# Eight left-over final products of a fused top-k attention and SMeLU kernel: three, three and two behind the next chunk's first pairs, instead of two behind each of four

## The chip, the cores and the metric

The kernel runs on one core of a Trainium2 chip. The metric is the device time of one execution in microseconds (us); lower is better. A profiled execution gives, beside its time, the span from its first to its last instruction and a trace of the engines: PE (TensorE, matmuls) with PEld (its weight loads), DVE (VectorE), ACT (ScalarE), POOL (GpSimd) and SP (SyncE, which issues the DMAs).

## What is computed

Eight batches of eight heads, 576 tokens, head size 64, all in fp32. First an attention that keeps, for each query, the 32 largest scores; then, on its 4608 rows of 512, a two-layer network with a smooth rectifier between the layers:

```python
scores = np.matmul(q, k.transpose(0, 1, 3, 2)) / np.sqrt(D)
kth = np.partition(scores, -32, axis=-1)[..., -32:-31]
scores = np.where(scores >= kth, scores, -1e9)
attn = softmax(scores)
x = np.matmul(attn, v)                    # brought to (4608, 512)
h = x @ w_in                              # w_in: 512 x 2048
g = np.where(h >= 1, h, np.where(h <= -1, 0, (h + 1) ** 2 / 4))
out = g @ w_out                           # w_out: 2048 x 512
```

## The kernel before

**Steps and chunks.** The attention goes in 144 steps; a step is one pair of heads of one tile of 128 queries (the 64 left-over queries of two batches share a tile). Four steps make a chunk of 128 rows of `x`, kept transposed in `xT`. There are 36 chunks, numbered here from 0 to 35; each then goes through the network.

**A step.** PE makes the scores (L327, tile `sp`), ACT scales and copies them to `s` (L329). DVE finds the 32nd largest score of each row with MAX8 and MATCH_REPLACE8 (L342 to L421), ACT makes the exponentials `e` in two halves (L363 `nmax`, L365), and DVE masks and sums them (L428). POOL divides by the sum (L381). ACT splits the weights into 16-bit halves (L458), a DMA writes them out as `rows` (L460), a transposing DMA brings them back as `wT` (L461), and PE multiplies them with the values (L475, L483, tile `po`), two steps after the step's own DVE work. ACT copies the result to `xT` (L488, L490). In the first dozen steps, while the network's weights are still being converted on ACT, DVE and POOL, and in the last two, PE transposes instead (L443, L449).

**A chunk in the network** (`mlp`, L499). Sixteen blocks f of 128 hidden units go in eight pairs x = 0 to 7 (`GROUP = 2`; the last chunk takes them singly). `hidden(x)` makes the **first products** of a pair, eight matmuls into the PSUM tile `ph` (three buffers, shared with `po`), which the trace shows as 16 records. ACT makes `r` (L512) and `g` (L519) of it, POOL finishes `g` (L524, L525, L526); `g` has eight buffers. `final(f)` makes one **final product** (L531): it adds block f of `g` times `w_out` into the PSUM tile `py`, and the trace shows two records. `py` has one buffer (`bufs=1`, L530). After final product 15, ACT copies `py` to `y` (L534) and SP sends it to `out` (L536).

**The order.** It is written by a planner when the program is built, and each engine goes through its own instructions in that order (`manual_schedule`). `mlp` is called when the values of a chunk's last step are issued and appends the chunk's work to the list `pending`: pairs x = 0 to 7, and the final products of pair x behind pair x + 4 (`LAG = 4`). So eight final products, 8 to 15, stand behind the last pair; they carry a mark (the fourth entry). When the next chunk comes, the marked ones that are still at the end of the list are taken off it into `behind` (L540 to L542) and mixed in between its first pairs. `advance` (L604) takes work from the head of the list, in seven slots a step: a pair costs 8 units, a final product 4, and a slot hands out a share that the step sets from the work that is left. In slot 2 come the values of two steps ago and the scores of two steps ahead; ACT's exponentials stand in slots 3 and 4, `halves` in slot 3, the `parts` copies for turned queries and keys in slot 1. ACT's copy to `y` and SP's DMA are issued with final product 15, wherever that falls.

Of the kernel before, what the change touches and what calls it, by code (L numbers as in the profile page):

```python
# [24 lines left out]
def kernel(  # L25
# [28 lines left out]
    GROUP = 2  # L54
# [59 lines left out]
    def needed(f, second):  # L114

        return (f // n_in) * (NK + n_in * n_out) + NK + (n_out * (f % n_in + 1) if second else 0)
# [54 lines left out]
    def run(ctx, paired):  # L171
# [327 lines left out]
        def mlp(xT, rows, pool, last):  # L499
            gs, group = {}, 1 if last else GROUP  # L500
            py = []

            def hidden(x):
                ph = ps.tile([P, group, P], F32, name="ph", tag="ph", bufs=3)
                for i in range(group):
                    f = x * group + i
                    for kk in range(NK):
                        nc.tensor.matmul(ph[:, i], w_in[:, kk, f * P:(f + 1) * P], xT[:, kk],  # L508
                                         start=(kk == 0), stop=(kk == NK - 1))

                r = pool.tile([P, GROUP, P], F32, name="r", bufs=2)[:, 0:group]
                nc.scalar.activation(r, ph, AF.Relu, bias=half, scale=0.5)  # L512
                gs[x] = g = pool.tile([P, GROUP, P], F32, name="g", bufs=2 * LAG)[:, 0:group]
                if last:
                    nc.vector.tensor_scalar(g, ph, -1.0, 0.0, ALU.add, ALU.max)
                    nc.scalar.activation(r, r, AF.Square)
                    nc.vector.scalar_tensor_tensor(out=g, in0=r, scalar=1.0, in1=g, op0=ALU.min, op1=ALU.add)
                    return
                nc.scalar.activation(g, ph, AF.Relu, bias=minus, scale=1.0)  # L519
                if converted < n_pieces and x % 2:  # L520
                    nc.scalar.activation(r, r, AF.Square)
                    nc.gpsimd.tensor_scalar(r, r, 1.0, 0.0, ALU.min, ALU.max)
                else:
                    nc.gpsimd.tensor_scalar(r, r, 1.0, 0.0, ALU.min, ALU.max)  # L524
                    nc.gpsimd.tensor_tensor(out=r, in0=r, in1=r, op=ALU.mult)  # L525
                nc.gpsimd.tensor_tensor(out=g, in0=r, in1=g, op=ALU.add)  # L526

            def final(f):
                if f == 0:
                    py.append(ps.tile([P, DM], F32, name="py", tag="py", bufs=1))  # L530
                nc.tensor.matmul(py[0], gs[f // group][:, f % group], w_out[:, f, :], start=(f == 0), stop=(f == NF - 1))  # L531
                if f == NF - 1:
                    y = (late or words).tile([P, DM], F32, name="y", bufs=1)
                    nc.scalar.copy(y, py[0])  # L534
                    for p0, p1, dst in rows:
                        nc.sync.dma_start(out=dst, in_=y[p0:p1])  # L536

            behind = []  # L540
            while pending and pending[-1][3]:
                behind.insert(0, pending.pop())  # L542
            for x in range(NF // group + LAG):
                if x < NF // group:
                    pending.append((NK * group, needed(x * group + group - 1, False), partial(hidden, x), False))
                if x < LAG:
                    for _ in range(min(GROUP, len(behind))):
                        pending.append(behind.pop(0)[0:3] + (False,))
                else:
                    for f in range((x - LAG) * group, (x - LAG + 1) * group):  # L550
                        pending.append((DM // P, needed(f, True), partial(final, f), x >= NF // group))
# [142 lines left out]
        def values_until(m):  # L694
            nonlocal valued, pe_time
            while valued < min(m, n):
                pe_time = max(pe_time, ready_at[valued]) + 1.25
                values(state[valued])
                state[valued] = None
                if valued in ready:  # L700
                    ch = ready[valued]
                    mlp(xTs[ch], rows_of(*chunks[ch]), mlp_pool, ch == len(chunks) - 1)
                valued += 1
# [117 lines left out]
```

## Time and profile before

| | us |
|---|---|
| median of 3 runs | 1583.9 (1581.3 to 1587.99) |
| profiled execution, its own time | 1578.63 |
| span of the profiled execution | 1576.8 |
| ACT busy in the span | 1162.1 |
| POOL busy in the span | 939.0 |
| first products on PE (L508), busy | 571.7 |
| final products on PE (L531), busy | 556.2 |
| scores on PE (L327, main form), busy | 163.0 |
| copies to `y` (L534), 36 of them, busy | 20.9 |

Busy time is time in which an engine executes an instruction; a matmul's end is modelled, so the start of the next one tells more than its end. A line of the timeline gives the start in us from the span's start, the length, the engine, the line of the kernel, the operation, the tiles written and read, the shapes and how many were merged; in brackets, if the engine was idle before it, for how long and what ended that. A line of the waits reads: who <- for what: us in all, how many times, the longest.

### The profile page before, as it was taken

To read this page: it belongs to the slowest core of one execution; us is meant where nothing else is said; L and a number is where in the kernel's file an instruction comes from. 1 tells how busy PE (TensorE), PEld (TensorE's weight loads), DVE (VectorE), ACT (ScalarE), POOL (GpSimd) and SP (SyncE) were. 2 spreads that over 40 slices of the span, in tenths; PEclk is the share of its full clock that TensorE was granted. 3 is DMA by queue.
4 is the path that set the end of the run, shared out by engine and by line. 5 is a ranking of instruction groups with operands and counts; after the bars stand their busy time and mean duration, and the time that the engine had idled before them with its cause. 6 is when DMAs were issued, how large, how long until landed. Compare 5 with 4: busy or idle time off the path is not lost.

```text
span 1576.8 us, 32399 instructions
## 1 busy us (share of the span) xinstructions
PE 1481.3 (94%) x10685; PEld 1056.7 (67%) x10685; DVE 1432.2 (91%) x4443; ACT 1162.1 (74%) x2278; POOL 939.0 (60%) x1376
## 2 busy tenths in 40 slices
PE   5587899999999999999999999999999999999998
PEld 4465667677777676666666766666777666777775
DVE  6999989999999999989998999989999999999912
ACT  5677667787778877777777877777778777777732
POOL 4766466566666556655666655566666665666630
PEclk6799999999999999999999999999999999999999
DMA  9433245866577767885576776676566866655610
GB/s 253 131 97 99 61 125 149 219 188 154 161 192 199 199 158 169 217 202 146 161 184 181 198 177 166 190 206 180 161 172 190 201 177 156 169 158 154 138 43 16
DMA packets 504626, 256.25 MB, mean 163 GB/s; under 512 B 451712, under 2 KB 459904, under 8 KB 504448
## 3 DMA queue, kind: packets, MB, share of 16 engines
q1 hardware_dynamic: 504448, 254.08, 61.0%
q8 instruction: 87, 1.43, 0.4%
q14 instruction: 91, 0.75, 0.2%
HBM read 62.91 MB, written 100.27 MB: 103 GB/s over the span
## 4 chain that ended last, share of the span: by engine, by line
PE 79%; ACT 8%; DMA 5%; DVE 4%; issue 2%; POOL 1%; ACTq 0%; DVEq 0%; POOLq 0%; SPq 0%
PE ph L508 29%; PE py L531 28%; PE sp L327 10%; PE po L475 9%; ACT halves L458 2%; DMA rows<-halves 2%; DMA wT<-rows 2%; PE pw L443 1%; PE po L483 1%; ACT e L365 1%; DVE bits L147 1%; DMA lines<-parts 1%; DVE more L349 1%; ACT s L329 1%; ACT r L512 1%
## 5 line engine op out<-in xcount | busy, mean ns | idle before, releaser
L508 PEld LDWEIGHTS ph<-xT,w_in 128*128 128x128 f32 x4608 | 555.8, 192 | 133.7 <-issue 100.4
L531 PE MATMUL py<-w_out,g 128*128 128x512 f32 x1152 | 556.2, 601 | 19.6 <-ACT y L534 19.6
L508 PE MATMUL ph<-xT,w_in 128*128 128x128 f32 x4608 | 571.7, 278 | 2.6 <-ACT xT L488 2.6
L524 POOL TENSOR_SCALAR r<-r 128x256 f32<-128x256 f32 x276 | 144.1, 522 | 500.1 <-ACT r L512 500.0
L349 DVE MATCH_REPLACE8 more<-tops,more 128x288 f32<-128x288 f32 x864 | 375.5, 438 | 0.0
L531 PEld LDWEIGHTS py<-w_out,g 128*128 128x128 f32 x1152 | 194.9, 191 | 170.0 <-issue 151.2
L458 ACT COPY halves<-e 128x1152 uint16<-128x1152 uint16 x260 | 285.1, 1142 | 8.2 <-DMA rows<-halves 6.4
L428 DVE SCALAR_TENSOR_TENSOR e<-s,kth,e 128x577 f32<-128x577 f32 x288 | 263.9, 945 | 23.0 <-ACT e L365 22.5
L512 ACT ACTIVATE r<-ph,half 128x256 f32<-128x256 f32 (+1 forms) x296 | 136.2, 460 | 144.4 <-PE ph L508 142.0
L526 POOL TENSOR_TENSOR g<-r,g 128x256 f32<-128x256 f32 x280 | 228.4, 816 | 22.0
L365 ACT ACTIVATE e<-s,nmax 128x576 f32<-128x576 f32 x288 | 222.5, 773 | 4.7
L381 POOL TENSOR_SCALAR e<-e,rz 128x576 f32<-128x576 f32 x260 | 226.0, 878 | 0.0
L329 ACT ACTIVATE s<-sp 128x576 f32<-128x576 f32 x288 | 173.3, 647 | 67.8 <-PE sp L327 63.8
L525 POOL TENSOR_TENSOR r<-r 128x256 f32<-128x256 f32 x276 | 197.2, 714 | 23.0
L327 PE MATMUL sp<-kT,qT 64*128 64x288 f32 x1024 | 163.0, 436 | 9.9 <-ACT kT L243 8.8
L475 PEld LDWEIGHTS po<-wT,v_in 128*64 128x64 f32 x2048 | 112.3, 138 | 77.7 <-issue 17.9
L475 PE MATMUL po<-wT,v_in 128*64 128x128 f32 x2048 | 144.6, 281 | 7.2 <-DMA wT<-rows 5.2
L342 DVE TENSOR_TENSOR more<-s 128x576 f32<-128x576 f32 x144 | 114.4, 794 | 40.1 <-ACT s L329 39.6
L519 ACT ACTIVATE g<-ph,minus 128x256 f32<-128x256 f32 x280 | 129.8, 464 | 0.0
L390 DVE MAX8 tops<-more 128x8 f32<-128x288 f32 x288 | 125.5, 443 | 0.0
L327 PEld LDWEIGHTS sp<-kT,qT 64*128 64x128 f32 x1024 | 90.3, 189 | 45.7 <-issue 16.7
L342 DVE TENSOR_TENSOR less<-s 128x576 f32<-128x576 f32 x144 | 118.9, 826 | 0.0
(95 smaller groups left out, 1469.9 us busy)
## 6 DMA issues: line engine op xcount, KB each, us to landing
rows<-halves SPq DMA_DIRECT2D x130, 576.0 KB, 3.0
raw<-in_moe_w_out_dram SPq DMA_DIRECT2D x52, 256.0 KB, 2.6
raw<-in_moe_w_in_dram SPq DMA_DIRECT2D x48, 256.0 KB, 2.9
lines<-parts SPq DMA_DIRECT2D x48, 256.0 KB, 2.6
q_in<-in_q_dram SPq DMA_DIRECT2D x32, 256.0 KB, 3.7
v_in<-in_v_dram SPq DMA_DIRECT2D x8, 1024.0 KB, 7.0
out_dram<-y SPq DMA_DIRECT2D x32, 256.0 KB, 3.1
kT<-in_moe_w_in_dram SPq DMA_DIRECT2D x16, 256.0 KB, 4.2
```

Of the source, the lines that this page charges most:

```text
L327: nc.tensor.matmul(o[:, a0 - c0:a1 - c0], qT[d, g, :], kT[d, g, k0:k0 + a1 - a0], start=True, stop=True)
L342: nc.vector.tensor_tensor(out=x, in0=s[:, :, 0:SH], in1=s[:, :, SH:S], op=op)
L349: nc.vector.match_replace(out=st["rest"][:, i, :], in_to_replace=eight(st["tops"], i, r - 8), in_values=src[:, i, :], imm_value=LOWEST)
L365: nc.scalar.activation(e[:, i, :], s[:, i, :], AF.Exp, bias=nmax[:, i:i + 1])
L381: nc.gpsimd.tensor_scalar(st["e"][:, i, :], st["e"][:, i, :], rz[:, i:i + 1], 1.0, ALU.mult, ALU.mult)
L428: nc.vector.scalar_tensor_tensor(out=st["all"][1][:, i, :], in0=st["all"][0][:, i, :], scalar=last[i], in1=st["all"][1][:, i, :], op0=ALU. ...
L458: nc.scalar.copy(halves[:, :, i * S:(i + 1) * S], st["e"][:, i, :].bitcast(U16).rearrange("p (k t) -> p t k", t=2))
L475: nc.tensor.matmul(po[j * D:(j + 1) * D], v_in[:, h, c, :] if c < NT else v_tl[0][:, h, :], wT[:, block(j, c)], start=(c == 0), stop=(c == ...
L508: nc.tensor.matmul(ph[:, i], w_in[:, kk, f * P:(f + 1) * P], xT[:, kk], start=(kk == 0), stop=(kk == NK - 1))
L525: nc.gpsimd.tensor_tensor(out=r, in0=r, in1=r, op=ALU.mult)
L526: nc.gpsimd.tensor_tensor(out=g, in0=r, in1=g, op=ALU.add)
L531: nc.tensor.matmul(py[0], gs[f // group][:, f % group], w_out[:, f, :], start=(f == 0), stop=(f == NF - 1))
```

## The change

One number in `mlp`. The left-over final products are put behind the next chunk's first pairs at most three to a pair, not two:

```diff
                 if x < LAG:
-                    for _ in range(min(GROUP, len(behind))):
+                    for _ in range(min(GROUP + 1, len(behind))):
                         pending.append(behind.pop(0)[0:3] + (False,))
```

With eight left over, the list that the planner works through (H for a pair of first products, F for a final product, a dash for the old chunk's) turns from

```
before: H0 F8' F9'      H1 F10' F11'      H2 F12' F13'  H3 F14' F15'  H4 F0 F1  H5 F2 F3 ...
after:  H0 F8' F9' F10' H1 F11' F12' F13' H2 F14' F15'  H3            H4 F0 F1  H5 F2 F3 ...
```

The copy to `y` and its DMA go with F15'. Where the planner has already done some of the eight when the next chunk comes, fewer are left to be mixed in, and the last of these pairs get fewer of them or none.

## The prediction

> **What bounds the kernel now.** I read the busy times of the page, then busy time by stretches, then TensorE's waits, then the timelines of TensorE and ScalarE around one wait. Columns of the second fence: stretch, length, busy time (and instructions) of PE, PEld, DVE, ACT, POOL, then granted clock, DMA share, GB/s.
>
> ```profile
> PE 1481.3 (94%) x10685; PEld 1056.7 (67%) x10685; DVE 1432.2 (91%) x4443; ACT 1162.1 (74%) x2278; POOL 939.0 (60%) x1376
> ```
>
> ```profile
> 550.00:1000.00 450.00, 432.71 (x3196) 305.94 (x3197) 418.04 (x1309) 341.06 (x646) 272.24 (x397) 1.00 0.69 178
> 1300.00:1500.00 200.00, 200.00 (x1503) 141.62 (x1500) 192.44 (x611) 153.43 (x292) 129.43 (x184) 1.00 0.59 154
> ```
>
> From 1300 to 1500 PE has no gap at all, while DVE has 7.6 us free. A step (one pair of heads of one query tile) there lasts 9.61 us by the starts of its score products, and PE's own pieces fill it: two pairs of first products (1.79 us each, from start to next start), four final products (0.86 each), values 1.25, scores 1.17, sum 9.44, and the rest is some 0.17 of change-over. So PE's work sets the pace, and a gap of PE in the steady part is time of the kernel unless PE later finds another engine late. From 550 to 1000 PE lacks 17.3 us. TensorE's waits (total, times, longest) say to what:
>
> ```profile
> PE py L531 <- ACT y L534: 19.6, 13, 2.8
> PE po L475 <- DMA wT<-rows: 5.2, 4, 1.7
> ```
>
> The first is the one accumulator `py`: final product 0 of a chunk overwrites it, so it waits until ScalarE has copied the last chunk's sum to `y`. The 13 single waits, from the timeline, by the chunk whose sum is copied: chunk 0 2.51, 9 2.20, 10 0.21, 11 0.72, 12 to 14 1.72 each, 15 1.06, 16 1.05, 17 0.68, 18 2.79, 19 0.61, 27 2.60; ten of them lie between 545 and 965. One of them on PE and on ACT:
>
> ```profile
> 750.52 2.05 PE L508 MATMUL ph<-xT,w_in 128*128 128x128 f32 x16
> 752.41 1.88 PE L531 MATMUL py<-w_out,g 128*128 128x512 f32 x4
> 754.13 1.95 PE L508 MATMUL ph<-xT,w_in 128*128 128x128 f32 x16
> 757.79 0.67 PE L531 MATMUL py<-w_out,g 128*128 128x512 f32 x1 [1.72 <-ACT y L534]
> ```
>
> ```profile
> 753.40 0.20 ACT L363 ACTIVATE nmax<-tops 128x2 f32<-128x2 f32 x1
> 753.63 0.78 ACT L365 ACTIVATE e<-s,nmax 128x576 f32<-128x576 f32 x1
> 754.32 2.19 ACT L458 COPY halves<-e 128x1152 uint16<-128x1152 uint16 x2
> 756.41 0.77 ACT L365 ACTIVATE e<-s,nmax 128x576 f32<-128x576 f32 x1
> 757.09 0.56 ACT L534 COPY y<-py 128x512 f32<-128x512 f32 x1
> ```
>
> The last final product (the second half of the x4; each product has two records) is through at 754.14, one pair of first products follows, and that pair, 1.79 us, is all the cover there is. The copy takes only 0.56, but it stands in ScalarE's queue behind the attention's burst: `e`, two `halves`, `e`.
>
> **The change, part by part.** Nothing is added or removed: 1152 records of final products, 36 copies, the same DMAs. In the middle chunks eight products are left over (six or seven for chunks 28 to 33, by walking through the planner's loop with its own costs and due times; for the kernel before this gives the order of first, final, value and score products that the trace shows).
>
> *(1) Cover of the copy.* Before, one pair stands between product 15 and the next product 0; after, two (pairs 3 and 4). The cover grows by 1.79 us. Each wait w becomes max(0, w - 1.79): 2.51 to 0.72, 2.20 to 0.41, 2.79 to 1.00, 2.60 to 0.81, the other nine to 0. Left: 2.9 us; saved: 19.6 - 2.9 = 16.7 us. As the copy moves up with product 15, it also changes places on ScalarE: by the walk it is issued before the burst for chunks 12 to 23, and for chunk 27 ahead of the `parts` copies, one of which started 3.1 us late, for its DMA, and made the 2.60. So these lose even the rest. For chunks 0 and 9 it still stands behind `halves`: 2.10 us after product 15 in chunk 9 are `halves`, then 0.58 of `y`, and the place after gives about 0.8 left there and 1.9 in chunk 0. Sum of the rest that way 2.7, so both ways about 2.8.
>
> *(2) Two pairs of first products in a row.* They need two of the three `ph` buffers. Their readers (L512, L519) end at least 3.7 us before the buffer is taken again from 160 to 1300 (smallest distance 1.6 later on). The trace has the pattern already, in chunk 33, for which only six products of chunk 32 were left:
>
> ```profile
> 1470.54 1.88 PE L531 MATMUL py<-w_out,g 128*128 128x512 f32 x4
> 1472.26 3.73 PE L508 MATMUL ph<-xT,w_in 128*128 128x128 f32 x32
> 1475.92 1.09 PE L475 MATMUL po<-wT,v_in 128*64 128x128 f32 x16
> ```
>
> The x32 are pairs 3 and 4, and no idle time stands before or behind them. Cost 0. If that cover failed, it would be one wait of up to 0.9 us (r and g of one pair on ACT) a chunk.
>
> *(3) Final products earlier, pairs 1 to 3 later.* Products 10 to 15 come up to 1.79 us earlier. They read `g`, and the closest one in the trace starts 9.9 us after POOL wrote its `g`: cost 0. Pairs 1 to 3 come up to 1.72 later; their `g` is read much later still. POOL's chain for a pair (0.52 + 0.71 + 0.82) moves with them, and POOL is busy 60%.
>
> *(4) Scores and values beside them.* Because the planner hands out work by cost, values and scores of some steps shift: by the walk, 0.93 us earlier in nine (1.79 in one more) and 0.86 to 1.79 later in seventeen, in ten stretches of one to four steps, then level again. Later scores delay DVE, which has about 0.36 us a step to spare (7.6 us in 21 steps) and sheds that within a few steps. Taken as 0, at worst once 0.86 for each of ten stretches (1.79 for one), 9.5 us.
>
> *(5) The queues passed.* `out_dram<-y` (SP, 0.37 us to issue, 3.0 to land) moves up, in chunks 12 to 19 past `rows<-halves` and its transpose. It waits for `y`, which ScalarE now makes before `halves`, so SP's next DMA waits for ScalarE anyway: 0. ScalarE waits in `y` for product 15 and holds what is behind it: that ends 0.86 or 1.72 us after the scores, whose own copies take 1.19, so up to 0.5 us in chunks 12 to 16. 0 on the path, at worst 3.
>
> *(6) What is late next.* Values start when the transposed weights have landed. The trace's landings lie 2 to 5 us ahead of most value products, but PE's waits for `y` have helped: a step's values come four steps after its scores, with one wait in between. Without it the distances between 545 and 1000 shrink by that wait. Six steps there had under 1.4 us: 55 (waiting 1.94 for a late `parts`), 56 and 57 (0.13 ahead), 60 (1.34), 61 (waiting 1.74), 72 (waiting 1.30). Step 61 would give back up to 1.7, 72 1.1, 55 and its neighbours 0.2 to 0.9: about 3 us, bounds 0 and the whole 16.7 (if the attention's chain itself can't go faster). I take 3, since from 1300 to 1500 the same work ran at 9.61 a step with no wait of PE, mostly 2 to 5 us ahead.
>
> **Sum.** 19.6 - 2.8 - 3 = 13.8 us. The profiled execution took 1578.63 (span 1576.8 and 1.8 around it) and becomes 1564.8. The runs' median is 1583.9, 5.3 above it; the same 13.8 off gives **1570**.
>
> **A rule against it.** PE's 94% against DVE's 91% is no proof by itself, since the ends of matmuls are modelled; what I trust are the starts. The Trainium skill (Perfetto Trace Analysis, Identifying the Most-Contended Engine) says to judge TensorE by its weight loads' busy share and the arithmetic done, not by matmul busy time. By that rule PE stands at 67%, DVE at 91% would be the engine to relieve, and the change would be worth about 0: 1583.9. The row from 1300 to 1500 speaks for PE: no gap there, and DVE not full.
>
> **Rivals.**
> *A, more comes back* (0.20): nothing is given back at the values, and scores that come sooner take away DVE's waits for `s` (39.6 us, 34 times in all). 19.6 or a little more: 1563. For it: PE never waits for values from 1300 to 1500. Against: step 61.
> *B, the wait only changes its name* (0.13): PE is early at `py` because the attention chain (DVE, ScalarE's burst, transposes) is the slower one there; then values wait for the transposes instead. For it: `PE po <- DMA wT` exists, and from 470 to 508 DVE is busy 38.00 of 38.00. Against: in that same stretch PE keeps 9.61 a step. Gain 0 to 5: about 1581. That the planner evens the new order out, so that the change does not reach product 0, ends here too; the walk speaks against it.
> *C, slower* (0.05): the copy, issued before the burst in chunks 12 to 23, holds ScalarE's queue while PE is still at product 15, and exponentials, `halves`, transposes and so values come late. The longest wait of `y` for PE before is 3.6 us; 12 chunks at 3.6 cost 43, less 16.7: some 1610. It breaks even at 1.4 us a chunk. My estimate for these is up to 0.5.
>
> **How the numbers follow.** My forecast has 0.62. A and the forecast are faster by over 0.5% (under 1576.0; half a per cent is about what a measurement can tell from no change), B within it but for a sliver on the fast side, C slower: faster 0.83, same 0.12, slower 0.05. The range runs from A to the fast edge of B: 1562 to 1579.
>
> **What would show it.** `PE py <- ACT y` falls from 19.6 to under 5, in no more than four waits; in chunk 14, 18 and 27 product 0 follows its pair at once; PE's gaps from 550 to 1000 shrink from 17.3 to about 8; `PE po <- DMA wT` grows by about 3. Wrong would be: that row growing by over 12 (B), or `ACT y <- PE py` (9.7 us now) rising past 25 with DVE's waits for `e` (C).

## The result, and the profile after

Over six runs each, the median falls from 1583.44 to 1562.53 us (1559.9 to 1565.3): ratio 0.9869, 95% interval 0.9848 to 0.9891. The profiled execution took 1560.56 (span 1558.8) and stands 18.1 us below that of before.

Stretches of the changed kernel, columns as in the prediction:

```profile
550.00:1000.00 450.00, 443.69 (x3307) 314.69 (x3304) 437.31 (x1347) 350.37 (x664) 283.74 (x406) 1.00 0.70 185
1300.00:1500.00 200.00, 198.46 (x1523) 142.77 (x1521) 185.28 (x577) 147.75 (x288) 126.21 (x182) 1.00 0.57 149
```

From 550 to 1000 PE now lacks 6.3 us, not 17.3. TensorE's waits:

```profile
PE po L483 <- DMA wT<-rows: 5.5, 3, 2.8
PE sp L327 <- DMA qTt<-lines: 4.3, 3, 2.9
PE py L531 <- ACT y L534: 1.0, 2, 0.8
```

The wait for `y` has gone from 19.6 to 1.0. What is left of it is 0.83 behind chunk 0 and 0.20 behind chunk 9. The other two rows are what PE waits for now. The second is new (before, such a row stood at 0.2 us, for `qT`). The first has not grown: before, these waits were 2.0 under this line and 5.2 under L475, which has 1.0 now. All of PE's idle time after the first 160 us sums to 35.8 us before and 18.3 after; the difference is 17.5 of the 18.0 by which the span got shorter. This is the hand-over from chunk 14 to 15, on PE and on ACT:

```profile
742.09 1.13 PE L531 MATMUL py<-w_out,g 128*128 128x512 f32 x2
743.05 3.73 PE L508 MATMUL ph<-xT,w_in 128*128 128x128 f32 x32
746.62 0.59 PE L531 MATMUL py<-w_out,g 128*128 128x512 f32 x1
```

```profile
743.25 0.58 ACT L534 COPY y<-py 128x512 f32<-128x512 f32 x1 [0.34 <-PE py L531]
743.73 0.21 ACT L363 ACTIVATE nmax<-tops 128x2 f32<-128x2 f32 x1
743.97 0.78 ACT L365 ACTIVATE e<-s,nmax 128x576 f32<-128x576 f32 x1
744.65 2.19 ACT L458 COPY halves<-e 128x1152 uint16<-128x1152 uint16 x2
746.75 0.77 ACT L365 ACTIVATE e<-s,nmax 128x576 f32<-128x576 f32 x1
```

Product 15 (the x2) ends, ScalarE copies at once, and the burst comes behind the copy. Before, the copy stood behind the same burst. The x32 are pairs 3 and 4 in a row, and product 0 follows them with no idle time.

### The profile page after: what moved, and what is told of

It reads as the page before. It is cut to its first block, busy times and chain, and to the rows that moved or that the text cites. A ratio compares the mean times of both kernels' runs of the same rounds, so it can differ in the third digit from the quotient of the medians.

```text
span 1558.8 us, 32420 instructions
## 1 busy us (share of the span) xinstructions
PE 1480.7 (95%) x10685; PEld 1057.5 (68%) x10685; DVE 1441.2 (92%) x4443; ACT 1159.7 (74%) x2278; POOL 947.1 (61%) x1376
## 3 DMA queue, kind: packets, MB, share of 16 engines
q8 instruction: 87, 1.43, 0.4%
## 4 chain that ended last, share of the span: by engine, by line
PE 81%; DMA 7%; ACT 6%; DVE 3%; issue 2%; SPq 1%; ACTq 0%; DVEq 0%
PE ph L508 30%; PE py L531 29%; PE sp L327 10%; PE po L475 9%; DMA wT<-rows 2%; DMA rows<-halves 2%; PE pw L443 1%; PE po L483 1%; ACT halves L458 1%; DMA lines<-parts 1%; ACT s L329 1%; DVE bits L147 1%; ACT e L365 1%; DVE more L349 1%; DMA qTt<-lines 1%
## 5 line engine op out<-in xcount | busy, mean ns | idle before, releaser
L508 PEld LDWEIGHTS ph<-xT,w_in 128*128 128x128 f32 x4608 | 552.1, 192 | 122.0 <-issue 90.1
L508 PE MATMUL ph<-xT,w_in 128*128 128x128 f32 x4608 | 567.0, 277 | 1.8 <-ACT xT L488 1.2
L531 PE MATMUL py<-w_out,g 128*128 128x512 f32 x1152 | 550.1, 600 | 1.0 <-ACT y L534 1.0
L428 DVE SCALAR_TENSOR_TENSOR e<-s,kth,e 128x577 f32<-128x577 f32 x288 | 267.2, 959 | 9.0 <-ACT e L365 8.7
L381 POOL TENSOR_SCALAR e<-e,rz 128x576 f32<-128x576 f32 x260 | 233.1, 906 | 2.0 <-DVE rz L374 2.0
L475 PEld LDWEIGHTS po<-wT,v_in 128*64 128x64 f32 x2048 | 111.5, 137 | 73.8 <-ACT g L519 14.8
L475 PE MATMUL po<-wT,v_in 128*64 128x128 f32 x2048 | 143.8, 279 | 5.7 <-ACT g L519 1.5
```

The source lines that it names most:

```text
L381: nc.gpsimd.tensor_scalar(st["e"][:, i, :], st["e"][:, i, :], rz[:, i:i + 1], 1.0, ALU.mult, ALU.mult)
L428: nc.vector.scalar_tensor_tensor(out=st["all"][1][:, i, :], in0=st["all"][0][:, i, :], scalar=last[i], in1=st["all"][1][:, i, :], op0=ALU. ...
L475: nc.tensor.matmul(po[j * D:(j + 1) * D], v_in[:, h, c, :] if c < NT else v_tl[0][:, h, :], wT[:, block(j, c)], start=(c == 0), stop=(c == ...
```

## The experiments

Two explanations fit this result. **C**, as in step 1 of the prediction: one pair more of PE's work lies between product 15 and product 0 and covers 1.79 us of each wait. **Q**: PE does the same work ahead of product 0 in both orders, so it gets there no later; what counts is that ScalarE meets the copy earlier in its queue, ahead of the burst. A third, **O**: the products that come earlier, or the shifted scores and values, are worth something of their own. Theory T in the expectations is C and Q together, theory B is the prediction's rival B.

All experiments have plain DMAs in place of the transposing ones, in both orders. What they leave out is in the expectations of the base runs; ACT's copies ahead of these DMAs keep the words in their own order, which the edits below leave out. So what the runs show, they show for these kernels; that it holds for the real pair rests on how alike its times and waits are to those of the second base. The lines of these kernels stand a few further down (L532 is the final product, L535 the copy).

**First base: short packets (p_).** The edit beside the order:

```diff
-            rows = dram.tile([P, 2, 2 * S], U16, name="rows")
-            nc.sync.dma_start(out=rows, in_=halves)
-            nc.sync.dma_start_transpose(wT.bitcast(U16), rows.rearrange("p t k -> (p t) k"))
+            rows = dram.tile([P, 2 * BLOCKS, P + 2], U16, name="rows")[:, :, 0:P]
+            nc.sync.dma_start(out=rows, in_=halves.rearrange("p t k -> p (t k)").rearrange("p (c k) -> p c k", k=P))
+            nc.sync.dma_start(out=wT.bitcast(U16).rearrange("p c k -> p (c k)").rearrange("p (c k) -> p c k", k=P), in_=rows)
...
-            nc.sync.dma_start_transpose(dst.bitcast(U16), lines.rearrange("p t k -> (p t) k"))
+            nc.sync.dma_start(out=dst.bitcast(U16),
+                              in_=lines.rearrange("p t k -> (p t k)").rearrange("(p c k) -> p c k", p=P, c=NHP))
```

p_old (order of before):

> The order of before, with the transposing DMAs of keys, queries and weights replaced by plain DMAs of as many bytes in packets of 256 and 512 B: ACT copies the words in their own order, and nothing is transposed, so the attention of batches 2 to 7 and the values get untransposed operands and the output is not the reference's. PE, DVE, ACT and POOL do the same work in the same order. It is the base for the other p_ kernels. Theory T (PE sets the pace and product 0 waits for the copy to y behind ScalarE's burst): PE's waits for y stay, 14 to 24 us; the time is that of before or up to 15 us less, as waits for transposes go: 1568 to 1584.

p_new (order of after):

> The order of after, with the same plain DMAs as p_old. Theory T: PE's waits for y 0 to 4 us and 14 to 22 us less than p_old. Rival B of the prediction (the attention chain with its transposes is the slower one where PE is early): with lighter transposes the gain is not smaller either, so this run alone does not part them; the gain on top of p_old would then be nearer to 25.

p_3221 and p_2240 change the number of left-over products behind each pair on top of p_old:

```diff
-                    for _ in range(min(GROUP, len(behind))):
+                    for _ in range(min((3, 2, 2, 1)[x], len(behind))):
```

> As p_old, with the eight left-over products 3, 2, 2, 1 behind the next chunk's first four pairs: products 10, 12 and 14 come a pair earlier, product 15 and with it the copy to y stays behind pair 3 as in p_old. Theory T (only the place of the copy counts): PE's waits for y 14 to 24 us, time within 4 us of p_old. Rival O (the gain comes from products that come earlier, or from the shifted scores and values): a third to two thirds of the difference between p_old and p_new, 6 to 14 us less than p_old.

> As p_old, with the eight 2, 2, 4, 0: the first two pairs as in p_old, products 14 and 15 and the copy moved from pair 3 to pair 2. Theory T: PE's waits for y 0 to 4 us, time within 4 us of p_new. Rival O: at most half of the difference between p_old and p_new.

Measured: 2147.95, 2146.84, 2144.36 and 2147.50 us, 35% over before (p_old's interval 1.3477 to 1.3552), and the order makes no difference. I had meant these DMAs to weigh as much as the transposing ones; they became the bound (the share of q1, the DMA queue, in the time of the 16 engines is 95.3%, before 61.0%). So they tell nothing of C or Q. The expectations of time for p_old and p_new failed; those for p_3221 and p_2240 (within 4 us of p_old and of p_new) were met, but only because all four times are alike. All four waits for `y` came out over what Theory T gives: 81.5, 18.4, 62.7 and 29.8 us. What the runs do show is what rival B describes, with these DMAs as the slow part of the attention's chain. TensorE's waits in p_old, then in p_new:

```profile
PE po L476 <- DMA wT<-rows: 248.1, 80, 8.8
PE py L532 <- ACT y L535: 81.5, 16, 9.1
```

```profile
PE po L476 <- DMA wT<-rows: 294.2, 93, 9.3
PE py L532 <- ACT y L535: 18.4, 8, 4.9
```

The new order takes 63 us off the wait for `y`, the values' wait for the weights rises by 46, some more comes back at smaller waits, and the time stays. PE's idle time after 160 us falls by only 15 us (434.8 to 419.6), and its busy time rises by 12 (1651.6 to 1663.4); TensorE's granted clock was 0.877 and 0.874 in these two, 0.977 before. Where the attention's chain sets the pace, PE's wait for `y` is only the place at which PE waits.

**Second base: whole rows (c_).** The same, but `rows` as in the kernel before, and one plain DMA back:

```diff
-            nc.sync.dma_start_transpose(wT.bitcast(U16), rows.rearrange("p t k -> (p t) k"))
+            nc.sync.dma_start(out=wT.bitcast(U16).rearrange("p c k -> p (c k)"), in_=rows.rearrange("p t k -> p (t k)"))
```

> The order of before, with the transposing DMAs of queries, keys and weights replaced by plain DMAs of the same bytes in whole rows (512 B to 4.6 KB), so that the DMA engines do not become the bound as in the p_ kernels; nothing is transposed, so the attention of batches 2 to 7 and the values get untransposed operands. It is the base for the other c_ kernels. Theory T (PE sets the pace, and product 0 waits for the copy to y): PE's waits for y 14 to 24 us, hardly any wait for wT, time 1568 to 1582. Theory B (the attention chain is as slow as PE): with lighter DMAs the waits for y shrink or vanish.

> The order of after, with the plain DMAs of c_old. Theory T: PE's waits for y 0 to 4 us, and 14 to 21 us less than c_old: ratio 0.987 to 0.991. Theory B: within 5 us of c_old.

Measured: c_old 1566.68, c_new 1544.11; to before 0.9866 (0.9844 to 0.9889) and 0.9729 (0.9707 to 0.9750). The difference, 22.6 us, is about that of the real pair, and so are the waits, c_old's and then c_new's:

```profile
PE py L532 <- ACT y L535: 19.4, 13, 2.8
```

```profile
PE py L532 <- ACT y L535: 1.0, 2, 0.8
```

The same 13 hand-overs wait, with the same longest wait as before: this base has what is to be studied. Theory B falls for this load: the lighter DMAs neither shrank the wait nor ate the gain. The gain was 1.6 us over the upper end expected, and c_old 1.3 us under its range.

**Cover or place in the queue: c_copy_after_pair3.** c_new with the copy issued behind `r` and `g` of the next chunk's pair 3; PE's own order is that of c_new (`copy_out` does the four lines taken out).

```diff
+        held = []
...
                 nc.gpsimd.tensor_tensor(out=g, in0=r, in1=g, op=ALU.add)
+                if x == 3 and held:
+                    held.pop()()
...
                 if f == NF - 1:
-                    y = (late or words).tile([P, DM], F32, name="y", bufs=1)
-                    nc.scalar.copy(y, py[0])
-                    for p0, p1, dst in rows:
-                        nc.sync.dma_start(out=dst, in_=y[p0:p1])
+                    held.append(copy_out)
+                    if last:
+                        held.pop()()
```

> As c_new, order of after on PE; only the copy to y and its DMA are issued behind ScalarE's r and g of the next chunk's pair 3, so that nothing of the pairs moves past the copy, as in c_old. Theory C (step 1 of the prediction: one more pair of PE's work between product 15 and product 0 covers 1.79 us of each wait): PE's waits for y about 3 us, 1542 to 1548. Theory Q (what makes the copy late is its place in ScalarE's queue; the work of PE ahead of product 0 is the same in both orders, so PE gets there at the same time): waits for y 12 to 20 us, 1556 to 1568.

Measured: 1566.39 (ratio 0.9873, 0.9846 to 0.9901), the time of c_old. Its wait, then one hand-over on PE and on ACT:

```profile
PE py L538 <- ACT y L546: 18.6, 17, 4.0
```

```profile
703.18 3.73 PE L511 MATMUL ph<-xT,w_in 128*128 128x128 f32 x32
708.05 1.53 PE L538 MATMUL py<-w_out,g 128*128 128x512 f32 x3 [1.14 <-ACT y L546]
```

```profile
703.85 2.19 ACT L459 COPY halves<-e 128x1152 uint16<-128x1152 uint16 x2
705.94 0.77 ACT L366 ACTIVATE e<-s,nmax 128x576 f32<-128x576 f32 x1
706.62 0.45 ACT L515 ACTIVATE r<-ph,half 128x256 f32<-128x256 f32 x1
706.98 0.45 ACT L524 ACTIVATE g<-ph,minus 128x256 f32<-128x256 f32 x1
707.33 0.57 ACT L546 COPY y<-py 128x512 f32<-128x512 f32 x1
```

Two pairs lie between product 15 and product 0, and product 0 waits all the same: the copy stands behind the burst again. Expected were about 3 us of wait by C and 12 to 20 by Q. C falls, Q holds. The copy's place is not quite that of c_old: `r` and `g` of pair 3 are ahead of it in both, but here they come last, and from the start of `r` to the copy they take 0.71 us. If that is taken off each of the 17 waits, an estimated 8.8 us are left, still three times what C gives. Nor does the run make the earlier product 15 needless: the copy reads its sum, so without it the copy can't come earlier either. No run has the early place without the early product.

**Which of the moved products counts: c_2240 and c_3221.** The edits are those of the p_ kernels of the same numbers (2, 2, 4, 0 and 3, 2, 2, 1), on c_old.

> As c_old, with the eight left-over products 2, 2, 4, 0: the first two pairs as in c_old, only products 14 and 15, and with them the copy, moved from pair 3 to pair 2. Theories C and Q: waits for y 0 to 4 us, within 4 us of c_new, 1540 to 1548. Theory O (the gain comes from products that come earlier or from the shifted scores and values): at most half of the 22 us of c_new, 1555 or more.

> As c_old, with the eight 3, 2, 2, 1: products 10, 12 and 14 a pair earlier, product 15 and the copy behind pair 3 as in c_old. Theories C and Q: waits for y 14 to 22 us, within 4 us of c_old, 1562 to 1571. Theory O: a third to two thirds of the 22 us, 1552 to 1560.

Measured: c_2240 1546.44 (0.9740, 0.9711 to 0.9768), c_3221 1567.87 (0.9877, 0.9849 to 0.9905). Their waits for `y`, c_2240's first (c_3221 has one more, of 1.1 us, which its trace puts under POOL's `r`, though product 0 starts there as the copy ends):

```profile
PE py L532 <- ACT y L535: 1.4, 2, 0.8
```

```profile
PE py L532 <- ACT y L535: 15.9, 11, 4.0
```

Moving only products 14 and 15 a pair up gives the time of c_new, and moving three earlier ones while 15 stays gives nothing. O falls.

**The whole price: c_no_copy_old and c_no_copy_new.**

```diff
-                if f == NF - 1:
+                if f == NF - 1 and last:
```

> As c_old, with the copy to y and its DMA left out for all chunks but the last, so only the last chunk's rows are written; product 0 waits for nothing. It bounds what the wait can be worth in the old order, with 20 us of ScalarE's work and the output's DMAs taken away as well. Theories C and Q: time of c_new or a little less, 1538 to 1546. Theory O: the old order keeps a cost of its own, 1550 or more.

> As c_new, with the copy to y and its DMA left out for all chunks but the last (only the last chunk's rows are written). Theory Q (the only thing that the new order changes is when ScalarE gets to the copy): the same as c_no_copy_old, 1540 to 1546, and within 4 us of c_new. Rival R (the new order also saves or costs something of its own): more than 5 us away from c_no_copy_old, under 1538 or over 1549.

Measured: 1543.26 (0.9720, 0.9690 to 0.9750) and 1541.24 (0.9717, 0.9683 to 0.9751). Without copy and wait the old order is as fast as the new one, and neither is told apart from c_new. So the new order has neither cost nor profit of its own that can be seen, and it has taken what there was to take at this place.

**Earlier still: c_4400.** The numbers are (4, 4, 0, 0), on c_old.

> As c_old, with the eight left-over products 4, 4 behind the first two pairs, and pairs 2, 3 and 4 in a row; the copy comes another pair earlier. Theory Q: PE's waits for y 0 to 1 us; there is no more to gain than the 1 us that c_new still waits, and ScalarE has three pairs of r and g in a row, so 1542 to 1549, not faster than c_new by more than 2. Rival C (every further pair of cover is worth something): 1538 to 1541.

Measured: 1541.95 (0.9720, 0.9687 to 0.9753), and no wait of `py` for `y` at all. The time lies between the ranges of Q (from 1542) and of C (up to 1541). The 2 us to c_new are less than the intervals' width; whether this order is a little better is open. Three pairs in a row cost nothing that shows.

## Why the prediction was right, and where it was not

*What bounds the kernel* was read rightly: time saved at PE's waits came off the kernel nearly one for one (17.5 of 18.0 us). *A rule against it*: by the weight loads' share, which is one of the two measures that the Trainium skill (Perfetto Trace Analysis, Identifying the Most-Contended Engine) names for TensorE, DVE stood first, and the prediction made a gain of 0 of that. The share rose from 67% to 68%, and the measured gain is 1.3%, so for this kernel the stretch without a gap told more than that share.

*Step 1* had the right outcome by a wrong reason. The first of its two ways, each wait shortened by the 1.79 us of one more pair, fails: with that pair there and the copy's place put back, the 18.6 us return. The pair is no extra cover, because it has only changed sides with the products, and PE reaches product 0 after the same sum of work. The second way, the copy's new place ahead of or within the burst, is what happened. In chunks 0 and 9 the copy still stands behind `halves`, as the walk had it. The two ways gave 2.9 and 2.7 left, and it was 1.0: 0.83 and 0.20 in chunks 0 and 9, where the second way had 1.9 and 0.8. The first way's 0.72 and 0.41 lie nearer, but it also had 1.00 and 0.81 for chunks 18 and 27, where nothing is left; that the two sums agreed is luck. One reading is off, though no sum uses it: eleven of the 13 waits lie between 545 and 965, not ten.

*Step 2*, priced at 0, has small costs: PE waits 1.5 us for `g` at L475 and 0.6 at L508, which it did not before; L475 makes the values, which share the three buffers with the pairs. *Steps 3 and 5* stand: no final product waits for POOL, and ScalarE's wait in `y` for PE fell from 9.7 to 9.1 us, so rival C did not come. *Step 4* stands in the sum: DVE's waits did not grow.

*Step 6* was mis-sized: 3 us to be given back, at the values of steps 55, 61 and 72. There the waits did not grow: step 55 waits 1.43 (1.94 before, under another name), 61 and 72 no longer show any. All values together wait 9.2 us for transposes, `parts`, `g` and issue, before 10.9. The transposes' part of that, which was to grow by about 3, went from 7.2 to 6.5, so rival B did not come either. What did come back is 4.0 us at scores that wait for turned queries (`qTt`), a row that I had not thought of. With `xT` at 1.2 instead of 2.6 and the rest, 1.1 net. The sign of rival A shows here, DVE's waits of before and of after:

```profile
DVE more L342 <- ACT s L329: 39.6, 34, 4.3
DVE e L428 <- ACT e L365: 22.5, 23, 1.8
```

```profile
DVE more L342 <- ACT s L329: 27.3, 20, 3.9
DVE e L428 <- ACT e L365: 8.7, 11, 1.8
```

With PE earlier, DVE waits less for scores and exponentials, and the attention's chain keeps up with PE instead of holding it. That this is why steps 61 and 72 stopped waiting is argued, not shown; no run took it apart.

*The sum*: 13.8 forecast, 18.1 in the profiled executions. Step 1 gave 1.8 more, step 6 1.9 more, and 0.6 is rest. The medians differ by 20.9, and their interval (about 17 to 24 us) holds the 18.1. So the time, 1562.5, came out at the low edge of 1562 to 1579, half a microsecond inside it: near rival A's 1563, and what A said of step 6 (nothing given back at the values, shorter waits of DVE for `s`) is what the rows show. Of the 7.5 us between 1570 and 1562.5, 4.3 are in the terms just named, 2.8 lie between the profiled executions and the medians, and the rest is the median of before, 0.5 lower over six runs than over three. That the range held is in part luck.

*Open*: c_old and c_new differ by 25.3 us in their profiled executions (c_old's is the slowest of its four) and PE's idle time after 160 us by 18.3 (25.8 to 7.5). Of the other 7.0 us, 3.4 are the granted clock: in c_old it was 0.50 from 549.3 to 552.7 and from 1272.9 to 1276.3, right behind the waits of 1.95 and 2.39 us for `y`, and c_new has no such stretch between 169 and 1536. Whether such a wait brings this on is not shown; before has no such stretch behind its longest wait, which ended at 919.5. Another 1.3 us lie at the start: chunk 1's first pair begins at 169.5 in c_old and at 168.2 in c_new. Some 2 us are left, in the time of the same instructions on PE. Since a matmul's end is modelled, part of a wait may hide in it; I have not settled that.

## What to carry to other kernels

When an engine waits for a short instruction of another, look at what stands ahead of that instruction in its engine's queue, and issue it earlier; work put between the two on the waiting engine is no cover if it was only moved from before them. Ask then which engine sets the pace: the same edit was worth 1.3 to 1.4% where PE did, and nothing where the DMAs did, though the wait shrank by three quarters there.

## What the runs showed of the hardware

The DMAs of the p_ kernels, issue to landing in us, p_old and then c_old, the same 576 KB in 130 issues:

```profile
rows<-halves SPq DMA_DIRECT2D x130, 576.0 KB, 11.4
```

```profile
rows<-halves SPq DMA_DIRECT2D x130, 576.0 KB, 2.8
```

Written in pieces of 256 B at steps of 260 B, these bytes took four times as long to land as in whole rows. Much of that is queueing, as the DMA engines were full: the output's DMA, which has the same form in both kernels, went from 3.4 to 10.2.

```profile
out_dram<-y SPq DMA_DIRECT2D x32, 256.0 KB, 10.2
```

```profile
out_dram<-y SPq DMA_DIRECT2D x32, 256.0 KB, 3.4
```

Another measure is the DMA engines' busy time. For the same 254.07 MB, q1 took 95.3% of 2146.3 us in p_old (748192 packets) and 50.3% of 1567.2 us in c_old (182432 packets): by these figures an estimated 2.6 times as much, for writing in pieces and reading back in pieces together. The Trainium skill (DMA: Bandwidth & Descriptors, Why small descriptors are slow) puts the overhead of a packet of 256 B at 27%. Its section How a descriptor splits into AXI transactions says that where a descriptor starts off a 256 B border, bytes below its start are fetched and cost time though they are not used. Which part each has in the 2.6 times, no run shows.
